# Attention and two MLPs on one core: the last batch's local v loaded from block 71 on, and two of its sets one block later

## The chip, the cores and the metric

The kernel runs on one core of one Trainium2 chip. The metric is the device time in microseconds; lower is better. Before the change three runs took 889.38, 891.51 and 893.7 us, with a median of 891.51 us. One execution was profiled; it took 892.35 us.

## The reference

The program chains three layers in float32.

```python
# attention: q, k, v are (4 batches, 8 heads, 576 positions, 64)
scores = q @ k.T / 8
rel = pos[:, None] - pos[None, :]
mask_local = (rel >= 0) & (rel < 32)                         # heads 0 to 3
mask_strided = (rel >= 0) & (pos[None, :] % 32 == pos[:, None] % 32)  # heads 4 to 7
attn = softmax(where(mask, scores, -1e9)) @ v                # x: 2304 tokens x 512
x = ((x @ w_a) * (x @ w_b)) @ w_out                          # 512 -> 1536 -> 512
h = x @ w_in                                                 # 512 -> 2048
out = (h * sigmoid(h)) @ w_out2                              # 2048 -> 512
```

The weights come as 64-bit floats and are read as pairs of 32-bit words.

## The kernel before

**Precision.** TensorE multiplies in a reduced float32 form. Each operand is therefore split into a high part (a cast, on ScalarE) and a rest (a subtraction, on VectorE), and each product is made of three matmuls. The splits are lines 775 and 776 for weights (`w<-raw`) and 793 and 794 for activations (`h<-h`, `h<-g`).

**Blocks.** The 2304 tokens are cut into groups of 512. The first 104 blocks, each of 12 matmuls of 128x512, work on group 0 through the first MLP (phase A, blocks 0 to 35), group 1 through the first MLP (blocks 36 to 71) and group 0 through the second MLP (phase B, blocks 72 to 103). In phase B a block is either an up product "i" (`ring<-y,w`, line 783, into one of two PSUM banks called ring) or a down product "p" (`acc<-w,h`, line 1568): the order is i0, i1, i2, p0, i3, p1 and so on, to i15, p13, p14, p15. So block 74 is i2, block 79 is p2, block 82 is i6, block 83 p4. What follows behind block 103 is a Strassen-like scheme for the remaining groups, which the change does not touch.

**Weights.** During the blocks the 64-bit weights are loaded (`words`, 512 KB a piece), converted by GpSimd (line 728), ScalarE (lines 744 and 702) and VectorE (line 753) to float32 (`raw`), kept in device memory (line 768) and loaded again for later blocks (`raw<-kept...`, line 693, 256 KB a piece, seven blocks ahead of use).

**Attention in the gaps.** Batch 0 is computed in a start-up stage. Batches 1 to 3 are computed between the blocks. A batch has nine units: five local ones (0 to 4; heads 0 to 3) and four strided ones (5 to 8; heads 4 to 7). They go in four sets, TOGETHER = (0, 1), (2, 3, 4), (5, 6), (7, 8). A table PLAN gives for each batch the block at which its loads begin, the block at which each set starts, and a last block for loads that belong to the next batch. For a set that starts at block s with n units, the scores (line 467, `att<-kT,qT`) stand on TensorE ahead of block s + 2; mask, maximum (lines 479, 489) and exponentials (line 501) follow in blocks s + 2 on, one unit a block; the sums are inverted (lines 524, 528) on VectorE and the probabilities normalised (line 539) on GpSimd in block s + n + 2; the transposition ("turn", line 559) stands ahead of block s + n - 1 + 6, and the values (line 608, `att<-ptl,vl` or `att<-pt,vs`) one block later. A table TURN_AT replaces the 6 for single sets: before, 7 for the first and 5 for the last set of batch 3.

**Loads of the attention.** q and k of the local heads and of the strided heads (`qld`, `kld`, line 312, 144 KB a piece, read in pieces of 128 bytes), local v (`vl`, lines 366 and 376: two loads of 32 KB, four of 128 and four of 144, read in pieces of 256 bytes) and strided v (`vs`, line 396) are issued by SP, one at a time at the start of a block. The function `spread` (line 806) distributes n issues evenly over a range of blocks. There is one buffer for `vl`; it is free for batch 3 when the second set of batch 2 has made its values, ahead of block 56.

**Order.** All instructions are issued in the order in which the Python code records them, each engine runs its own in that order, and SP's queue holds the loads of weights and of attention alike. The pieces to look at are `load_vl` (line 362), `plan_attention` (line 802) and `block` (line 848).

Of the kernel before, what the change touches and what calls it, by code (L numbers as in the profile page):

```python
# [106 lines left out]
PLAN = {  # L107
    1: (0, [2, 10, 18, 26], 36),
    2: (37, [40, 47, 55, 62], 70),
    3: (70, [73, 81, 89, 96], 0),  # L110
}
TURN_AT = {(3, 0): 7, (3, 7): 5}

STILL = 3
BETWEEN = (1, 2, 1, 2, 3, 1, 2)
# [14 lines left out]
def attention_gated_mlp_silu_mlp(  # L130
# [671 lines left out]
    def plan_attention(batch, s0, first, end):  # L802

        add = lambda at, place, f, *a: plan.setdefault((at, place), []).append((f, a))

        def spread(loads, n, s0, s1):
            for m in range(n):
                add(s0 + m * (s1 - s0) // n, "load", next, loads, None)

        starts = {us[0]: s for us, s in zip(TOGETHER, first)}  # L810
        first1 = starts[NL]
        turn1 = first1 - 1
        for one in range(4):
            add(s0 + (one if batch.b > 1 else one // 2), "prepare", batch.transpose_qk, 0, one)
            add(turn1 - 4 + one + one // 2, "prepare", batch.transpose_qk, 1, one)
        spread(batch.load_qk(1), 9, s0 + (4 if batch.b > 1 else 2), turn1 - 7)
        spread(batch.load_vs(), 4 * TAKE + 5, s0 + 4 * (batch.b > 1), first1 + 3)
        for us, s in zip(TOGETHER, first):
            others = len(us) - 1
            turn = s + others + TURN_AT.get((batch.b, us[0]), 6)  # L820
            add(s + 2, "softmax", batch.sums, *us)
            add(s + 2, "tensor", batch.scores, *us)
            for n, u in enumerate(us):
                add(s + n - others, "prepare", batch.prepare, u)
                add(s + n + 2, "mask", batch.mask, u)
                add(s + n + 2, "mask", batch.largest, u)
                add(s + n + 2, "softmax", batch.softmax, u)
                add(turn, "turned", batch.turned, u)
            add(s + others + 3, "normalise", batch.guard, us[0])
            add(s + others + 3, "normalise", batch.invert, us[0])  # L830
            for u in us:
                add(s + others + 3, "normalise", batch.normalise, u)
            add(turn, "tensor", batch.turn, *us)
            add(turn + 1, "tensor", batch.values, *us)
            add(turn + 1, "store", batch.store, *us)
        after = Batch(batch.b + 1, False)
        if after.b < B:
            spread(after.load_qk(0), 9, turn1 + 2, end)
            spread(after.load_vl(), 10, first1 + 7, end)
        return after  # L840

    def background(at, *places):
# [35 lines left out]
    with tc.manual_schedule():  # L878
# [13 lines left out]
        after = Batch(1, False)  # L892
# [96 lines left out]
        sp, hs, late, ys = {}, {}, {}, {}  # L989
# [510 lines left out]
        for ph, g in PHASES:  # L1500
# [7 lines left out]
            for kind, j in half[ph]:  # L1508
                if batch.b < B and p == PLAN[batch.b][0]:
                    batch = plan_attention(batch, *PLAN[batch.b])  # L1510
# [119 lines left out]
```

## Time and profile before

| what | value |
| --- | --- |
| runs | 889.38, 891.51, 893.7 us |
| profiled execution | 892.35 us |
| its span, first to last instruction | 890.6 us |
| TensorE busy | 878.5 us, 99% of the span |
| VectorE, ScalarE, GpSimd busy | 637.3, 541.8, 161.4 us |
| mean granted clock of TensorE | 0.988 |

The span is 1.75 us shorter than the time of the same execution. A timeline has one engine's instructions in order of time; in brackets stands how long the engine was idle before an instruction, and what ended that idle time. SP does not compute: its rows are the issues of DMA transfers, and a row's length is that of the issue, not of the transfer.

### The profile page before, as it was taken

What the parts mean: (1) busy time and instruction counts of PE and PEld (TensorE: products, weight loads), DVE (VectorE), ACT (ScalarE), POOL (GpSimd) and SP (SyncE); (2) the same over time, 40 slices, a digit from 0 to 9 for tenths busy, and PEclk for the clock granted to TensorE, in tenths of its full rate; (3) what the DMA queues carried; (4) which work ended last, traced back from release to release, by engine and by line L of the source; (5) the groups of instructions that cost most, each with busy time, mean ns of one, the idle gap of its engine ahead of it and who ended that gap; (6) DMA issues with size and microseconds to landing.
All of it is one profiled execution on the core that took longest, in us unless ns stands there. A gap on an engine that the chain in (4) does not pass through costs nothing.

```text
span 890.6 us, 16104 instructions
## 1 busy us (share of the span) xinstructions
PE 878.5 (99%) x5859; PEld 731.4 (82%) x5866; DVE 637.3 (72%) x1177; ACT 541.8 (61%) x1294; POOL 161.4 (18%) x232
## 2 busy tenths in 40 slices
PE   8899999999999999999999999999999999999998
PEld 5578788888887788999888888888888888989887
DVE  4587877767667776788776668766777697766664
ACT  4679898777777656665444344655554565455553
POOL 5655664444443200100000000000000000000000
PEclk9599999999999999999999999999999999999999
DMA  9999999798999923664122222321121342321201
GB/s 182 219 233 281 290 283 296 222 286 275 308 283 296 312 88 95 190 188 145 47 72 57 62 71 71 112 78 59 59 73 49 96 164 71 126 65 51 81 0 71
DMA packets 152977, 133.77 MB, mean 150 GB/s; under 512 B 91522, under 2 KB 114690, under 8 KB 152898
## 3 DMA queue, kind: packets, MB, share of 16 engines
q1 hardware_dynamic: 143986, 108.59, 43.3%
q0 software_dynamic: 7424, 23.34, 7.2%
q8 instruction: 46, 0.75, 0.4%
q10 hardware_dynamic: 1488, 0.82, 0.3%
q14 instruction: 33, 0.27, 0.1%
HBM read 110.16 MB, written 22.54 MB: 149 GB/s over the span
## 4 chain that ended last, share of the span: by engine, by line
PE 90%; DVE 3%; DMA 2%; ACT 2%; issue 1%; SPq 1%; POOL 1%; DVEq 0%; POOLq 0%; ACTq 0%
PE ring L783 19%; PE acc L1169 13%; PE ring L1105 12%; PE att L1105 9%; PE ring L1169 7%; PE att L1169 7%; PE acc L1105 7%; PE acc L1540 6%; PE acc L1568 4%; PE att L608 1%; PE acc L887 1%; PE att L467 1%; PE acc L783 1%; DMA raw<-kepti 1%; PE att L559 1%
## 5 line engine op out<-in xcount | busy, mean ns | idle before, releaser
L1434 DVE TENSOR_TENSOR w<-raw,w 128x512 fp32r<-128x512 f32 (+1 forms) x164 | 103.3, 642 | 14.8 <-ACT w L1433 13.9
L783 PE MATMUL ring<-x1a,w 128*128 128x256 f32 (+1 forms) x480 | 99.0, 327 | 0.0
L1433 ACT CAST w<-raw 128x512 fp32r<-128x512 f32 (+1 forms) x164 | 93.1, 581 | 7.2 <-ACT w L1433 3.0
L1105 PE MATMUL ring<-L,w 128*128 128x512 f32 x360 | 87.8, 389 | 0.0
L1218 POOL DMA_DIRECT2D out_dram<-o x12 | 6.5, 546 | 407.8 <-DVE o L1217 398.9
L1105 PEld LDWEIGHTS ring<-L,w 128*128 128x128 f32 x360 | 67.6, 188 | 14.0
L1169 PE MATMUL acc<-w,h 128*128 128x512 f32 x288 | 78.5, 391 | 0.0
L783 PEld LDWEIGHTS ring<-x1a,w 128*128 128x128 f32 x480 | 71.5, 190 | 7.8
L1540 PE MATMUL acc<-h,w 128*128 128x512 f32 x288 | 70.5, 394 | 0.6 <-ACT h L793 0.4
L793 ACT CAST h<-h 128x512 fp32r<-128x512 f32 (+1 forms) x48 | 27.2, 566 | 72.0 <-DVE h L1142 40.5
L776 DVE TENSOR_TENSOR w<-raw,w 128x512 fp32r<-128x512 f32 x80 | 61.7, 775 | 10.9 <-ACT w L775 10.2
L1540 PEld LDWEIGHTS acc<-h,w 128*128 128x128 f32 x288 | 53.2, 188 | 12.3 <-ACT h L793 0.6
L1169 PEld LDWEIGHTS acc<-w,h 128*128 128x128 f32 x288 | 53.6, 188 | 9.4 <-DVE h L794 0.4
L728 POOL TENSOR_SCALAR raw<-words 128x512 f16<-128x512 uint8 x56 | 51.2, 915 | 42.7 <-DMA words<-in_moe_w_in_dram 9.2
L783 PE MATMUL ring<-x,w 128*128 128x512 f32 x240 | 58.0, 394 | 0.1
L1169 PE MATMUL acc<-h,w 128*128 128x256 f32 (+1 forms) x288 | 53.5, 336 | 0.0
L783 PEld LDWEIGHTS ring<-x,w 128*128 128x128 f32 x240 | 44.4, 188 | 10.2 <-DVE w L776 1.1
L1169 PE MATMUL ring<-w,h 128*128 128x512 f32 x192 | 52.0, 391 | 0.0
L775 ACT CAST w<-raw 128x512 fp32r<-128x512 f32 x80 | 49.6, 623 | 1.2 <-DMA raw<-kepti 1.2
L1169 PEld LDWEIGHTS acc<-h,w 128*128 128x128 f32 x288 | 45.2, 190 | 5.7
L794 DVE TENSOR_TENSOR h<-h,h 128x512 fp32r<-128x512 f32 (+1 forms) x48 | 30.6, 637 | 26.4 <-ACT h L793 26.4
L1169 PE MATMUL att<-w,h 128*128 128x512 f32 x192 | 49.3, 391 | 0.0
(264 smaller groups left out, 1918.3 us busy)
## 6 DMA issues: line engine op xcount, KB each, us to landing
raw<-keptp SPq DMA_DIRECT2D x64, 256.0 KB
words<-in_moe_w_out_dram SPq DMA_DIRECT2D x28, 512.0 KB
raw<-kepti SPq DMA_DIRECT2D x48, 256.0 KB
raw<-kepto SPq DMA_DIRECT2D x45, 256.0 KB
words<-in_moe_w_in_dram SPq DMA_DIRECT2D x16, 512.0 KB
raw<-keptb SPq DMA_DIRECT2D x32, 256.0 KB
raw<-kepta SPq DMA_DIRECT2D x31, 256.0 KB
words<-in_moe_w_a_dram SPq DMA_DIRECT2D x12, 512.0 KB
```

The costliest lines, as they stand in the source:

```text
L728: nc.gpsimd.tensor_scalar(out=halves_of(made[c], F16, 1), in0=bytes_of(words[c], 8, 7), scalar1=-TINY, scalar2=127.5 * TINY, op0=ALU.mult, ...
L775: nc.scalar.copy(out=o[:, 0], in_=t)
L776: nc.vector.tensor_tensor(out=o[:, 1], in0=t, in1=o[:, 0].bitcast(F32), op=ALU.subtract)
L783: nc.tensor.matmul(ps[:, :T], lhsT=w[:, wi, c * P:(c + 1) * P], rhs=x[:, xi, c, :T], start=(c == 0 and wi == 0 and xi == 0), stop=(c == CC ...
L793: nc.scalar.copy(out=o[:, 0, :T], in_=t32[:, :T])
L794: nc.vector.tensor_tensor(out=o[:, 1, :T], in0=t32[:, :T], in1=o[:, 0, :T].bitcast(F32), op=ALU.subtract)
L1105: nc.tensor.matmul(self.acc[acc], lhsT=w[:, wi, (2 * part + c) * P:(2 * part + c + 1) * P], rhs=x[:, xi, c], start=(begin and c == 0 and m ...
L1169: nc.tensor.matmul(o, lhsT=lhsT, rhs=rhs, start=(first and wi == 0 and xi == 0), stop=(last and wi == 1))
L1433: nc.scalar.copy(out=o[:, 0, cols], in_=t)
L1434: nc.vector.tensor_tensor(out=o[:, 1, cols], in0=t, in1=o[:, 0, cols].bitcast(F32), op=ALU.subtract)
L1540: nc.tensor.matmul(accs[d], lhsT=w[:, wi, d * P:(d + 1) * P], rhs=h[:, xi], start=(j == 0 and wi == 0 and xi == 0), stop=(j == N1 - 1 and ...
L1568: nc.tensor.matmul(accs[t][:, :DM], lhsT=h[:, xi, t * P:(t + 1) * P], rhs=w[:, wi, :], start=(j == 0 and wi == 0 and xi == 0), stop=(j == ...
```

## The change

Three things are edited. The second and the third set of batch 3 start one block later (81 to 82 and 89 to 90). The third set's turn comes five blocks behind instead of six, so it stays ahead of block 96 and its values ahead of block 97. The loads of batch 3's local v, which were spread over blocks 62 to 69, are spread from block 71 on, one a block to block 79 (two in block 71). Since the loads of strided q, k and v are spread up to a block that depends on the third set's start, some of these move back by a block too.

```diff
 PLAN = {
     1: (0, [2, 10, 18, 26], 36),
     2: (37, [40, 47, 55, 62], 70),
-    3: (70, [73, 81, 89, 96], 0),
+    3: (70, [73, 82, 90, 96], 0),
 }
-TURN_AT = {(3, 0): 7, (3, 7): 5}
+TURN_AT = {(3, 0): 7, (3, 5): 5, (3, 7): 5}
...
         if after.b < B:
             spread(after.load_qk(0), 9, turn1 + 2, end)
-            spread(after.load_vl(), 10, first1 + 7, end)
+            late = end + 1 if after.b == 3 else first1 + 7
+            spread(after.load_vl(), 10, late, late + 9 if after.b == 3 else end)
         return after
```

`first1` is the block at which the third set of the batch before starts (55), `end` its last block for loads (70). Lines behind the edit have numbers higher by one in the changed kernel. A small float32 matmul of the attention (lines 467 and 608) stands once in the order below and twice in the trace, so 40 rows of scores there are 80 in the timeline.

SP, blocks 77 to 79: the last k and strided-v loads around the words load of block 78, before.

```order
L674 DMA words<-in_moe_w_out_dram 128x1024
L693 DMA raw<-kepti_3062 128x512
L312 DMA kld<-in_k_dram 32x36x32
L396 DMA vs<-in_v_dram 18x10x64
L674 DMA words<-in_moe_w_out_dram 128x1024
L693 DMA raw<-keptp_3102 128x512
L312 DMA kld<-in_k_dram 32x36x32
L396 DMA vs<-in_v_dram 18x10x64
```

The same place in the changed order, up to the last load of local v.

```order
L396 DMA vs<-in_v_dram 18x10x64
L674 DMA words<-in_moe_w_out_dram 128x1024
L693 DMA raw<-kepti_3062 128x512
L376 DMA vl<-in_v_dram 64x9x64
L312 DMA kld<-in_k_dram 32x36x32
L396 DMA vs<-in_v_dram 18x10x64
L674 DMA words<-in_moe_w_out_dram 128x1024
L693 DMA raw<-keptp_3102 128x512
L376 DMA vl<-in_v_dram 64x9x64
L312 DMA kld<-in_k_dram 32x36x32
```

Ahead of each block's first load now stands one of local v; the last one, in block 79, stands behind the words and the raw load of block 78, and the k loads have moved back by one place.

TensorE, from the values of the first set (`vl` with `ptl_120` and `ptl_121`) to the scores of the second, before.

```order
L608 MATMUL att<-ptl_120,vl 64x32 x16
L608 MATMUL att<-ptl_121,vl 64x32 x16
L783 MATMUL ring<-y,w 128x512 x12
L467 MATMUL att<-kT,qT 32x64 x40
L1568 MATMUL acc_3799<-w,h 128x512 x3
L1568 MATMUL acc_3800<-w,h 128x512 x3
L1568 MATMUL acc_3801<-w,h 128x512 x3
L1568 MATMUL acc_3802<-w,h 128x512 x3
```

The same place in the changed order.

```order
L608 MATMUL att<-ptl_120,vl 64x32 x16
L608 MATMUL att<-ptl_121,vl 64x32 x16
L783 MATMUL ring<-y,w 128x512 x12
L1569 MATMUL acc_3791<-w,h 128x512 x3
L1569 MATMUL acc_3792<-w,h 128x512 x3
L1569 MATMUL acc_3793<-w,h 128x512 x3
L1569 MATMUL acc_3794<-w,h 128x512 x3
L467 MATMUL att<-kT,qT 32x64 x40
```

Block 83, the twelve matmuls into the four acc banks, has moved from behind the second set's scores to in front of them.

VectorE, from the second unit's mask and maximum in the third set to its reciprocal, before: `g` is the gate of a weight block, `su` and `rs` the sums and their reciprocals.

```order
L479 SCALAR_TENSOR_TENSOR sm<-att,mask_str 128x162 x2
L489 TENSOR_REDUCE nm<-sm 128x6
L776 TENSOR_TENSOR w<-raw,w 128x512
L1532 SCALAR_TENSOR_TENSOR g_4643<-th,ring 128x512
L794 TENSOR_TENSOR h<-g_4643,h 128x512
L524 TENSOR_SCALAR su<-su 128x12
L528 RECIPROCAL rs<-su 128x12
L776 TENSOR_TENSOR w<-raw,w 128x512 x2
```

The same place in the changed order.

```order
L1533 SCALAR_TENSOR_TENSOR g_4632<-th,ring 128x512
L794 TENSOR_TENSOR h<-g_4632,h 128x512
L479 SCALAR_TENSOR_TENSOR sm<-att,mask_str 128x162 x2
L489 TENSOR_REDUCE nm<-sm 128x6
L776 TENSOR_TENSOR w<-raw,w 128x512
L524 TENSOR_SCALAR su<-su 128x12
L528 RECIPROCAL rs<-su 128x12
L776 TENSOR_TENSOR w<-raw,w 128x512
L1533 SCALAR_TENSOR_TENSOR g_4689<-th,ring 128x512
```

The mask and the maximum have moved from ahead of block 92's gate and split to behind them; the reciprocal still stands ahead of block 94's gate, now close behind the maximum.

## Rows read from the trace of the kernel before

**Rows 1.** The page: busy time of TensorE, DMA share in 40 slices, instruction queue.

```profile
PE 878.5 (99%) x5859; PEld 731.4 (82%) x5866; DVE 637.3 (72%) x1177; ACT 541.8 (61%) x1294; POOL 161.4 (18%) x232
...
DMA  9999999798999923664122222321121342321201
...
q8 instruction: 46, 0.75, 0.4%
```

**Rows 2.** Windows of the span: first column the stretch, second its length, then PE busy.

```profile
0.00:45.00 45.00, 39.36 (x562) 25.60 (x568) 23.03 (x78) 25.35 (x118) 27.28 (x49) 0.77 0.93 202
...
550.00:890.00 340.00, 336.90 (x1555) 287.31 (x1553) 241.46 (x437) 181.99 (x355) 4.31 (x8) 1.00 0.24 77
```

**Rows 3.** Timeline of PE: start, length, line, output<-inputs, count, idle time before it.

```profile
271.24 3.06 PE L783 MATMUL ring<-y,w 128*128 128x512 f32 x12 [0.75 <-DVE g L1532]
...
286.07 2.88 PE L1568 MATMUL acc<-w,h 128*128 128x512 f32 x12
...
289.65 2.57 PE L783 MATMUL ring<-y,w 128*128 128x512 f32 x10 [0.25 <-DVE w L776]
...
295.36 1.14 PE L608 MATMUL att<-ptl,vl 64*64 64x32 f32 x64
...
299.37 0.76 PE L467 MATMUL att<-kT,qT 64*32 64x64 f32 x49
301.01 0.46 PE L467 MATMUL att<-kT,qT 64*32 64x64 f32 x31 [0.88 <-issue]
...
317.85 0.71 PE L559 MATMUL att<-ident,prs 128*128 128x128 f32 x5
```

**Rows 4.** Timeline of ACT, 262 to 312 us.

```profile
266.71 0.62 ACT L775 CAST w<-raw 128x512 fp32r<-128x512 f32 x1 [1.20 <-DMA raw<-kepti]
```

**Rows 5.** Timeline of SP's DMA issues, 225 to 325 us.

```profile
236.93 2.33 SPq L366 DMA_DIRECT2D vl<-in_v_dram  x2
...
260.47 0.49 SPq L693 DMA_DIRECT2D raw<-kepti  x1
...
262.33 0.60 SPq L376 DMA_DIRECT2D vl<-in_v_dram  x1
...
274.62 1.22 SPq L312 DMA_DIRECT2D qld<-in_q_dram  x2
...
292.16 0.55 SPq L674 DMA_DIRECT2D words<-in_moe_w_out_dram  x1
292.81 0.38 SPq L693 DMA_DIRECT2D raw<-keptp  x1
```

**Rows 6.** Timeline of POOL, 225 to 365 us.

```profile
298.26 0.83 POOL L728 TENSOR_SCALAR raw<-words 128x512 f16<-128x512 uint8 x1 [1.40 <-DMA words<-in_moe_w_out_dram]
...
313.87 1.99 POOL L539 TENSOR_TENSOR prs<-prs,rs 128x256 f32<-128x256 f32 x3 [7.71 <-DVE rs L528]
337.84 2.14 POOL L539 TENSOR_TENSOR prs<-prs,rs 128x324 f32<-128x324 f32 x2 [21.97 <-DVE rs L528]
```

**Rows 7.** Windows with and without local-v loads: the last two columns are DMA share and GB/s.

```profile
237.00:263.00 26.00, 26.00 (x233) 21.25 (x234) 16.02 (x28) 19.20 (x54) 10.31 (x14) 1.00 1.08 310
264.00:274.00 10.00, 9.25 (x41) 7.23 (x39) 8.05 (x12) 6.77 (x12) 3.82 (x6) 1.00 1.08 333
274.00:293.00 19.00, 18.75 (x145) 15.04 (x144) 13.46 (x25) 13.49 (x37) 7.40 (x9) 1.00 0.99 248
```

**Rows 8.** The tile vl: its transfers from issue to landing.

```profile
DMA to landing us min/median/max: 3.2/5.4/8.0
```

**Rows 9.** Timeline of DVE, 317 to 366 us.

```profile
337.44 0.23 DVE L528 RECIPROCAL rs<-su 128x12 f32<-128x12 f32 x1
```

**Rows 10.** Timeline of PE, 317 to 372 us.

```profile
325.47 0.92 PE L467 MATMUL att<-kT,qT 64*64 64x54 f32 x48
...
340.06 0.82 PE L559 MATMUL att<-ident,prs 128*118 128x128 f32 x6
```

## The prediction

> **What bounds the kernel now.** I read the page first: TensorE is busy 878.5 us of a span of 890.6, 99% [rows 1], so no change can gain more than the 12 us in which it is idle. The windows of the span say where those are: 45.00 - 39.36 = 5.6 us in the start-up and 340.00 - 336.90 = 3.1 us behind 550 us [rows 2], both out of the change's reach. The timeline of TensorE then shows three holes in the stretch that the change touches: 0.75, 0.25 and 0.88 us, 1.88 us together [rows 3]. That sum is the most that the change can give, 0.2% of the time; what it can cost is not bounded in this way.
>
> The first hole has a history. A load of a piece of the weights issued at 260.47 us, between two of the local-v loads [rows 5], lets ScalarE wait 1.20 us and start its cast only at 266.71 [rows 4], 6.2 us after the issue. VectorE is late behind it, frees the ring bank late, and TensorE waits 0.75 us at 271.24 [rows 3]. The second hole, 0.25 us, ends with a split weight, so again with the feeding of weights. The third, 0.88 us, falls in the middle of the second set's 80 score matmuls: 49 run, then nothing that the profile can name, then 31 [rows 3]. It stands behind 64 value matmuls and 49 score matmuls that took 1.14 and 0.76 us, so many instructions in little time, and the page shows an instruction queue of 46 packets with 0.75 MB [rows 1], 16 KB each, that shares the DMA engines. I take it to be late code.
>
> The DMA digits show that the transfers, too, are near their limit in slices of 22.3 us up to the fourteenth, that is to 312 us [rows 1]. The coarser windows agree: 310 GB/s from 237 to 263 us, while batch 3's ten local-v loads are issued, 333 from 264 to 274, and only 248 at a DMA share of 0.99 from 274 to 293, where eight q and k loads with their 128-byte pieces go out [rows 7].
>
> **Part 1: local v goes from blocks 62 to 69 to blocks 71 to 79.** Ten issues leave SP between 236.93 and about 263 us [rows 5] and take the same ten places among the loads of the first blocks of phase B. What is removed: two of 32 KB, four of 128 and four of 144, 1152 KB in all, ahead of the weights. At 310 GB/s that is 3.8 us of DMA time, more than the 1.20 us by which ScalarE was late, so I take away the whole first hole, -0.75, and the second with it, -0.25 (at worst both stay: 0).
>
> What it adds is a wait. The values of the first set read all of local v with their first eight matmuls. Before, it landed some 30 us ahead. Now its last load is an instruction of block 79, three blocks ahead of the values. SP does not issue it when TensorE begins block 79. SP runs in its own order: behind the words load issued at 292.16 and the raw load at 292.81 [rows 5] comes the last local-v load in the changed order, while TensorE starts those values at 295.36 [rows 3], and without the first two holes at 295.36 - 1.00 = 294.36. Queued behind that wait on TensorE are the values themselves, blocks 82 and 83 and the second set's scores: all of its work, so a microsecond of wait is a microsecond of time.
>
> When does the load land? The row nearest to it is the words load of 292.16: GpSimd, waiting for it for 1.40 us, starts at 298.26 [rows 6], 6.1 us after the issue. In the changed order the last local-v load is the second one behind that same load, and up to there the queue has carried the same transfers as before, less one k load (144 KB, 0.46 us at 310 GB/s), which goes out later. If the DMA engines stay saturated, the order of transfers doesn't change when the last of them is done, so 298.2 - 0.5 = 297.7 us, and TensorE waits 297.7 - 294.36 = +3.3 us. From below: SP runs ahead by the 1.20 us that ScalarE no longer loses, issues at 292.16 - 1.2 = 291.0, and the load needs 3.2 us, the shortest shown for this tile [rows 8]: 294.2, no wait, 0. From above: the engines idle before 274 us, where the weights alone don't fill them, and the six loads from block 74 on (832 KB, less 144 KB of k) go at the 248 GB/s of that stretch: 2.8 us later than 293.2, where the raw load's issue ends, and 6.1 us to land: 302.1, a wait of 7.7. I take 3.3, since its row lies next to the load in the queue, and keep 0 and 7.7. Weights that SP issues behind local v come later by up to the same amount, but TensorE's wait gives them that time back.
>
> A rule of the Trainium skill speaks against the new place ("DMA: Bandwidth & Descriptors", section "Why small descriptors are slow (HBM only)"): a 256-byte piece costs 11 cycles instead of 8. Local v is read in 256-byte pieces, so by that rule the six loads from block 74 on would cost about a quarter more, as an estimate 0.6 us, and the wait would be 3.9 in place of 3.3. The trace agrees only in part: with these loads in the queue the rate was 310 GB/s against 333 without [rows 7], 7% less.
>
> **Part 2: the second set one block later.** Same matmuls, another place: block 83 of 24 weight matmuls now runs between the values and the 80 scores. If the third hole is late code, the 2.7 us of that block give the fetch its time, and a wait for local v does so as well: -0.88 (it stays: 0). The rest of the set keeps its distance of seven blocks from scores to values; GpSimd's normalising began at 313.87 and took 1.99, and the turn came at 317.85 [rows 6, 3], so 2.0 us of slack, and both move by the same block. The turn and the values also move one block: 0.
>
> The Trainium skill ("Runtime: NRT & Kernel Launch", section "Instruction fetch mechanics") holds the cost of crossing into the next 16 KiB of code to be mostly hidden. By that the hole is not code, and would stay: the sum would be 0.88 higher. The size per packet agrees with the page of the profile; the hole, with no other releaser, does not look hidden, so I keep -0.88.
>
> **Part 3: the third set one block later, its turn where it was.** The distance from start to turn shrinks by a block. Before, scores began at 325.47, the reciprocal at 337.44, GpSimd normalised from 337.84 to 339.98, and TensorE turned from 340.06 [rows 9, 6, 10]: already with almost nothing to spare. But the chain had waits in it that the later start eats up: VectorE did the reciprocal behind a weight block's gate and split. Laid out from the durations, scores now end 2.7 us later, the two softmaxes follow at 330.2 and 336.0, the reciprocal ends near 338.4, and GpSimd is done by 340.6 in place of 339.98. TensorE needs the second half only 0.3 us into the turn. That is +0.3; from below 0, from above one whole block, 2.7, if a gate slips ahead of the softmax.
>
> **Sum.** -0.75 - 0.25 - 0.88 + 3.3 + 0.3 = +1.7 us. The profiled execution took 892.35 us, so 894.1; it lay 0.84 above the median of the runs, 891.51, and on that scale I predict 893.2.
>
> **The rivals.**
> - No wait at the values: SP is so far ahead by block 79 that local v lands by 294.4. For it, SP's pace before 274 us is set by free buffers and not by the DMA, so it starts the stretch unburdened; against it, the raw load of 292.81, the last issue of block 78, is 6.7 us behind the start of block 79 on TensorE at 286.07 [rows 5, 3]. Then -1.88 + 0.3: 889.9.
> - Slower than before: the wait for the last local-v load grows to 6 us or more, since eight q and k loads and now six local-v loads are squeezed into 19 us at 248 GB/s [rows 7]. It decides from a wait of 1.88 - 0.3 = 1.6 us on whether the kernel loses at all, and from about 6 whether the loss can be told. With 7: -1.88 + 7 + 0.3 = +5.4, 896.9.
> - The third set's turn slips by a block, with local v in time: -1.88 + 2.7, 892.3. For it, 0.1 us of slack before [rows 6, 10]; against it, the layout above.
> - The change does not do what it says: the holes stay (late code and late weights are found at other places), and local v lands in time: 891.5.
>
> **How the numbers follow.** Forecast 0.42 (its own range 891.4 to 895.9, for waits from 1.5 to 6); no wait 0.30; longer wait 0.14; third set 0.06; nothing 0.08. What differs by under 0.5%, 4.5 us, can't be told from no change in a measurement of this kernel. Only the longer wait goes beyond that, most of it: slower 0.13. A gain of 4.5 us is more than the holes hold; 0.03 is left for what I have not seen. Same: 0.84. The range goes from no wait, less 0.9 for the scatter of the runs, 889.0, to the longer wait at 897.0.
>
> **What would show it.** Right: the profile after has a TensorE wait in front of the first set's values, its releaser a DMA or nothing named, of 1.5 to 6 us, no hole near 270 us and none in the second set's scores. Part 1 is wrong if those values follow block 81 without a hole; part 2 if the scores still break off; part 3 if TensorE waits over 1 us for GpSimd at the third set's turn. A gain of more than 1.9 us would mean that time came from outside these blocks.

## The result and the profile after

The changed kernel takes 899.91 us (median of 6 runs, 899.22 to 902.77) against 891.13 for the kernel before (6 runs); the ratio is 1.0098, with an interval of 1.0082 to 1.0114. It is 8.8 us slower. The prediction said 893.2, in a range up to 897.0.

The profiled execution took 902.77 us with a span of 901.0, the slowest of the six, so its parts add up to a little more than the medians: its span is 10.4 us longer than the one before. The timeline of TensorE after shows nearly all of it in one place (start, length, line, output<-inputs, count, idle time before):

```profile
286.10 2.88 PE L1569 MATMUL acc<-w,h 128*128 128x512 f32 x12
...
289.66 2.59 PE L783 MATMUL ring<-y,w 128*128 128x512 f32 x10 [0.23 <-DVE w L776]
...
295.40 0.42 PE L608 MATMUL att<-ptl,vl 64*64 64x32 f32 x12
298.73 0.30 PE L608 MATMUL att<-ptl,vl 64*64 64x32 f32 x2 [2.91 <-DMA vl<-in_v_dram]
304.08 1.70 PE L608 MATMUL att<-ptl,vl 64*64 64x32 f32 x50 [5.05 <-DMA vl<-in_v_dram]
305.71 4.80 PE L783 MATMUL ring<-y,w 128*128 128x512 f32 x12
310.35 2.91 PE L1569 MATMUL acc<-w,h 128*128 128x512 f32 x12
313.19 1.04 PE L467 MATMUL att<-kT,qT 64*32 64x64 f32 x80
...
350.10 1.17 PE L559 MATMUL att<-ident,prs 128*118 128x128 f32 x6
```

The values of the first set begin at 295.40, before at 295.36 [rows 3], although a hole of 0.75 us ahead of them is gone: in this execution TensorE is busy for 38.90 of the first 45 us and was for 39.36, so the start-up took that gain away. After six of them (twelve rows) TensorE waits 2.91 us for a load of local v, and after the seventh 5.05 us for the next: 8.0 us. Then everything is slow for a while: the last 50 value matmuls take 1.70 us, and the weight block i6 4.80, where such a block took 3.06 at 271.24 before [rows 3]. From the start of the values to the start of i6 it is 10.31 us and was 1.07; from there to what follows i6 (block p4 after, the scores before) 4.64 and was 2.94. That is 9.24 + 1.70. The scores at 313.19 no longer break off, and what lies between i6 and the third set's turn is 0.94 us shorter. So from the values to that turn: +9.24 + 1.70 - 0.94 = +10.0 of the 10.4. The turn itself takes 0.35 us more, 1.17 against 0.82 [rows 10].

The windows of 2 us after (last three columns: granted clock of TensorE, DMA share, GB/s) say why the work behind the wait is slow:

```profile
296.00:298.00 2.00, 0.00 (x0) 0.00 (x0) 1.32 (x2) 0.62 (x1) 0.89 (x2) 1.00 1.11 302
298.00:300.00 2.00, 0.30 (x2) 0.19 (x2) 0.98 (x2) 1.80 (x3) 0.44 (x1) 0.83 0.59 105
300.00:302.00 2.00, 0.00 (x0) 0.00 (x0) 0.69 (x1) 0.00 (x0) 0.01 (x1) 0.50 0.96 365
...
306.00:308.00 2.00, 2.00 (x5) 1.53 (x5) 0.69 (x1) 1.99 (x5) 0.00 (x0) 0.50 1.17 248
...
310.00:312.00 2.00, 2.00 (x11) 1.61 (x10) 0.69 (x1) 0.70 (x2) 0.00 (x0) 1.00 0.98 316
```

TensorE stands still from 296 to 304 apart from two matmuls; the granted clock falls to 0.50, that is 1.2 GHz, from 300 us on, and is back at 1.00, 2.4 GHz, by 310. The values and i6 run in between: 1.3 + 1.7 = 3.0 us on top of the waits of 8.0.

SP's issues after show where the last load of local v stands in time:

```profile
267.49 0.32 SPq L693 DMA_DIRECT2D raw<-keptp  x1
267.87 1.35 SPq L366 DMA_DIRECT2D vl<-in_v_dram  x2
...
274.62 0.61 SPq L376 DMA_DIRECT2D vl<-in_v_dram  x1
...
292.34 0.61 SPq L376 DMA_DIRECT2D vl<-in_v_dram  x1
...
293.72 2.98 SPq L396 DMA_DIRECT2D vs<-in_v_dram  x1
296.81 1.23 SPq L674 DMA_DIRECT2D words<-in_moe_w_out_dram  x1
...
299.52 0.61 SPq L376 DMA_DIRECT2D vl<-in_v_dram  x1
```

The words load of block 78 goes out at 296.81 and was issued at 292.16 before; the last local-v load follows it, at 299.52, and TensorE goes on at 304.08, 4.6 us later. Landing itself took no longer than thought: the issue is late. Ahead of the words load, the issue of one strided-v load takes 2.98 us. It is no single event: from 274.62 on, the lengths of SP's issues add up to 23.2 of the 24.8 us until the raw load in front of the last local-v load is out. So SP hardly pauses for buffers there; it is its issues that take the time.

The coarse windows that answer to [rows 7]:

```profile
237.00:263.00 26.00, 26.00 (x233) 20.98 (x232) 15.62 (x29) 19.21 (x54) 10.58 (x15) 1.00 1.04 337
264.00:274.00 10.00, 10.00 (x46) 8.18 (x44) 7.69 (x12) 7.29 (x13) 2.56 (x5) 1.00 0.72 208
274.00:293.00 19.00, 18.77 (x145) 15.01 (x143) 13.73 (x25) 13.49 (x37) 6.91 (x9) 1.00 1.02 268
293.00:312.00 19.00, 11.04 (x95) 8.79 (x94) 6.69 (x10) 8.23 (x18) 2.66 (x4) 0.73 1.00 267
```

Without local v in front, the engines move 337 GB/s up to 263 us, and then, from 264 to 274, only 208 where there were 333. Up to 267.49 SP stands still for 6.6 us, until VectorE frees a buffer for a raw load, and the first local-v load is queued behind that raw load. From 274 on they are at a share of 1.02 but at 268 GB/s, little more than the 248 of before.

### The profile page after: what moved, and what is told of

Same layout as the page of the kernel before. It is cut to its first block, busy times and chain, and to the rows that moved or that the text cites. A ratio compares the mean times of both kernels' runs of the same rounds, so it can differ in the third digit from the quotient of the medians.

```text
span 901.0 us, 16101 instructions
## 1 busy us (share of the span) xinstructions
PE 881.8 (98%) x5859; PEld 733.7 (81%) x5866; DVE 637.6 (71%) x1177; ACT 541.9 (60%) x1294; POOL 161.3 (18%) x232
## 4 chain that ended last, share of the span: by engine, by line
PE 86%; ACT 5%; DVE 4%; DMA 3%; issue 1%; SPq 1%; POOL 1%; ACTq 0%; DVEq 0%; POOLq 0%
PE ring L783 17%; PE acc L1170 13%; PE ring L1106 12%; PE att L1106 9%; PE ring L1170 7%; PE att L1170 7%; PE acc L1106 7%; PE acc L1541 6%; PE acc L1569 3%; PE att L608 1%; ACT w L775 1%; ACT prs L501 1%; PE att L467 1%; PE acc L783 1%; DMA kld<-in_k_dram 1%
## 5 line engine op out<-in xcount | busy, mean ns | idle before, releaser
L1435 DVE TENSOR_TENSOR w<-raw,w 128x512 fp32r<-128x512 f32 (+1 forms) x164 | 103.4, 642 | 14.8 <-ACT w L1434 14.1
```

Source lines behind the costliest of these rows:

```text
L1435: nc.vector.tensor_tensor(out=o[:, 1, cols], in0=t, in1=o[:, 0, cols].bitcast(F32), op=ALU.subtract)
```

## The experiments

Theory A is that the wait for the last local-v load is the whole loss. It is split into A1 (the load is late because SP comes to it late, behind q and k) and A2 (the DMA engines are full, whoever issues, and whenever), and theory C adds the clock. Rival B puts a part of the loss on the sets that were moved. Ratios are against the kernel before on the same chip. Block 79 begins at 282.93 us in the earliest of these traces and at 286.10 in the latest, so an issue is placed by its distance from the start of block 79 in its own trace: 13.4 us for the last local-v load of the change (299.52 - 286.10).

**Only local v late.** PLAN and TURN_AT as before, the edit of `spread` as in the change.

```diff
-    3: (70, [73, 82, 90, 96], 0),
+    3: (70, [73, 81, 89, 96], 0),
...
-TURN_AT = {(3, 0): 7, (3, 5): 5, (3, 7): 5}
+TURN_AT = {(3, 0): 7, (3, 7): 5}
```

> Local v is loaded from block 71 on as in the change; the sets start where they did before (81, 89, six blocks to the third turn). Theory A (the wait of the first set's values for the last local-v load is the whole loss): the two waits in front of those values stay, 6 to 8 us together, and the time is 898 to 901 us, 8 to 10 us above before. Rival B (a part of the loss comes from the sets that start later): under 896 us.

Measured: 901.03 us, ratio 1.0109 (1.0088 to 1.0129). TensorE's timeline at the first set's values:

```profile
293.34 0.42 PE L608 MATMUL att<-ptl,vl 64*64 64x32 f32 x12
298.58 0.42 PE L608 MATMUL att<-ptl,vl 64*64 64x32 f32 x2 [4.81 <-DMA vl<-in_v_dram]
302.76 1.70 PE L608 MATMUL att<-ptl,vl 64*64 64x32 f32 x50 [3.76 <-DMA vl<-in_v_dram]
...
309.06 1.04 PE L467 MATMUL att<-kT,qT 64*32 64x64 f32 x80
```

The waits are 4.81 and 3.76 us, 8.6 together. This edit alone gives the whole loss; B is out. The second set's 80 scores run in one piece here too, although they stand right behind i6 as before.

**Only the sets moved.** Local v in blocks 62 to 69.

```diff
-            late = end + 1 if after.b == 3 else first1 + 7
-            spread(after.load_vl(), 10, late, late + 9 if after.b == 3 else end)
+            late = first1 + 7
+            spread(after.load_vl(), 10, late, end)
```

> The second and third set of batch 3 start one block later with the five-block turn as in the change; local v is loaded in blocks 62 to 69 as before. Theory A: no wait for local v; the holes near 270 and 289 us stay as in the kernel before, the break in the second set's scores is gone (-0.9 us), the third turn waits under 0.5 us: 889.5 to 891.5 us. Rival B: 894 us or more, with a wait of TensorE at one of the two moved sets.

Measured: 889.70 us, ratio 0.9981 (0.9967 to 0.9994): a little faster than before. The timeline of TensorE has the first set's values and the second's scores without a break, and the third set's turn with one:

```profile
270.49 3.02 PE L783 MATMUL ring<-y,w 128*128 128x512 f32 x12 [0.30 <-DVE g L1533]
...
294.59 1.14 PE L608 MATMUL att<-ptl,vl 64*64 64x32 f32 x64
...
301.32 1.04 PE L467 MATMUL att<-kT,qT 64*32 64x64 f32 x80
...
338.91 0.54 PE L559 MATMUL att<-ident,prs 128*118 128x128 f32 x3 [0.15 <-POOL prs L539]
```

The 80 scores run in one piece, as forecast for part 2, and GpSimd holds the second half of the third turn for 0.15 us, as sized in part 3. The hole at 270 us is there again, 0.30 us this time.

**The values a block later.**

```diff
-TURN_AT = {(3, 0): 7, (3, 5): 5, (3, 7): 5}
+TURN_AT = {(3, 0): 8, (3, 5): 5, (3, 7): 5}
```

> The change, but the first set of batch 3 is turned eight blocks behind its start instead of seven, so that its values stand ahead of block 83 and not 82. Theory A: block 82 now runs during the wait, which gets one block (2.7 us) shorter: 896 to 898 us. If the late load is itself held up by what TensorE does there (buffers that blocks 82 and on free), it lands later too and the gain is under 1 us: 899 us or more.

Measured: 897.61 us, ratio 1.0076 (1.0056 to 1.0095), 2.3 us below the change, as theory A expected, though the intervals of the two ratios overlap.

```profile
298.11 0.69 PE L608 MATMUL att<-ptl,vl 64*64 64x32 f32 x14 [2.97 <-ACT ptl L568]
301.17 1.70 PE L608 MATMUL att<-ptl,vl 64*64 64x32 f32 x50 [2.37 <-DMA vl<-in_v_dram]
```

TensorE still waits 2.97 and 2.37 us, 5.3 in place of 8.0: one block of work less in the wait. The second wait is for local v. The first is for the copies of the turned probabilities, and ScalarE's timeline says why they are late:

```profile
296.00 0.62 ACT L775 CAST w<-raw 128x512 fp32r<-128x512 f32 x1 [2.21 <-DMA raw<-kepti]
...
297.70 0.63 ACT L568 COPY ptl<-att 128x256 f32<-128x256 f32 x2
```

The cast in front of them waited 2.21 us for a piece of the weights. So it is not local v alone that comes late: what SP issues behind it is late as well, and here that shows.

**The late loads issued by GpSimd.** At the same blocks, past SP's queue.

```diff
+        def issue(loads, queue):
+            feed[0] = queue
+            next(loads, None)
+            feed[0] = nc.sync
...
-            spread(after.load_vl(), 10, late, late + 9 if after.b == 3 else end)
+            spread(after.load_vl(), 10, late, late + 9 if after.b == 3 else end, nc.gpsimd if after.b == 3 else nc.sync)
```

> The change, with the ten late local-v loads of batch 3 issued by GpSimd instead of SP, at the same blocks. Theory A1 (the load is late because SP issues it late, behind the q, k and strided-v loads in its queue): issued near the start of block 79 and landed about 5 us later, it meets the values: no wait or under 1.5 us, 889 to 892 us. Rival A2 (the DMA engines are full, whoever issues): the values still wait 4 us or more, 895 to 900 us.

Measured: 895.19 us, ratio 1.0048 (1.0029 to 1.0066). GpSimd's last issue of local v, and TensorE at block 79 and at the values:

```profile
290.09 0.80 POOL L376 DMA_DIRECT2D vl<-in_v_dram  x1
```

```profile
283.80 2.88 PE L1574 MATMUL acc<-w,h 128*128 128x512 f32 x12
...
295.21 0.30 PE L608 MATMUL att<-ptl,vl 64*64 64x32 f32 x2 [1.62 <-DMA vl<-in_v_dram]
297.00 1.49 PE L608 MATMUL att<-ptl,vl 64*64 64x32 f32 x50 [1.50 <-DMA vl<-in_v_dram]
```

The last load is issued 6.3 us behind the start of block 79, 7.1 us nearer to it than in the change, yet it lands only by 297.0, 6.9 us after its issue, and TensorE waits 3.1 us. Neither forecast fits whole: the time is at the lower end of A2's range, the wait below its 4 us. Past SP's queue 4.8 of the 8.0 us of wait go. That fits a load that is late because of its place in that queue, but this run does not say how much of the wait comes from there, since the edit changes the transfers too: the page counts the 1.2 MB of these loads under queue q0, software_dynamic, in 512 packets, where the change has them under q1, hardware_dynamic, in 4768.

**The q and k loads behind local v.** The eight loads of strided q and k go out in blocks 80 to 84, behind the last local-v load.

```diff
-        spread(batch.load_qk(1), 9, s0 + (4 if batch.b > 1 else 2), turn1 - 7)
+        spread(batch.load_qk(1), 9, s0 + (10 if batch.b == 3 else 4 if batch.b > 1 else 2), turn1 - (4 if batch.b == 3 else 7))
```

> The change, with the eight loads of batch 3's strided q and k issued in blocks 80 to 84 instead of 74 to 81, behind the last local-v load. Theory A1 (the q and k loads with their 128-byte pieces ahead in SP's queue are what makes the last local-v load late): it is issued by 291 us and landed by 296, the wait falls under 2 us: 889 to 893 us, unless the transposes of the late q then wait. Rival (the words and raw loads, which wait for free buffers, hold SP): SP issues the last local-v load as late as in the change, 297 us or later: 897 us or more.

Measured: 890.98 us, ratio 1.0006 (0.9994 to 1.0018). The same ten late local-v loads, in the same blocks, and no loss. SP's last local-v issue, TensorE at block 79 and at the values, and the two windows of the transfers:

```profile
290.76 0.61 SPq L376 DMA_DIRECT2D vl<-in_v_dram  x1
```

```profile
285.16 2.88 PE L1569 MATMUL acc<-w,h 128*128 128x512 f32 x12
...
294.54 0.43 PE L608 MATMUL att<-ptl,vl 64*64 64x32 f32 x14
295.64 1.00 PE L608 MATMUL att<-ptl,vl 64*64 64x32 f32 x50 [0.68 <-DMA vl<-in_v_dram]
```

```profile
264.00:274.00 10.00, 10.00 (x105) 8.09 (x104) 8.30 (x13) 6.85 (x13) 2.12 (x3) 1.00 0.61 187
274.00:293.00 19.00, 18.71 (x106) 15.10 (x89) 13.57 (x25) 14.24 (x37) 7.01 (x10) 1.00 1.05 309
```

SP issues the last load 5.6 us behind the start of block 79, 7.8 us nearer to it than in the change, and TensorE waits 0.68 us for it. From the fifth of the ten local-v loads, at 273.74 (274.62 in the change), to the raw load in front of the tenth SP is issuing for 8.7 of 17.0 us, where it was 23.2 of 24.8. The five strided-v loads in that stretch take 2.3 us to issue and took 7.4. What makes an issue longer is not shown; the share of the engines, 1.05 here and 1.02 in the change, does not tell the two apart. With local v and weights and without q and k, the engines move 309 GB/s from 274 to 293 us in place of 268. From 264 to 274 they are as idle as in the change, 187 GB/s. So the idle time ahead of 274 us does not make the load late by itself; the six q and k loads in front of it do. Whether that comes from their 128-byte pieces or from six more loads in the queue, no run separates.

**Local v from block 68, 65 and 70.** Three kernels, with the sets moved as in the change.

```diff
-            late = end + 1 if after.b == 3 else first1 + 7
+            late = 68 if after.b == 3 else first1 + 7
```

The others have 65 and `end` (70) in place of 68.

> The change, with batch 3's local v issued in blocks 68 to 76 instead of 71 to 79. In the trace after, SP issues what stands at block 76 at about 285 to 289 us, and a load needs 5 to 6 us. Theory A1 (SP's lateness grows from block 74 on with the q and k loads): the last load lands at 290 to 294, before the values at 295: 889 to 891.5 us, no wait. Rival A2 (the DMA engines' load in this stretch sets it, three blocks change little): a wait of 3 us or more, 894 us or more.

> The change, with batch 3's local v issued in blocks 65 to 73, still later than the 62 to 69 of before. Theory A: no wait for local v, and the two small holes of weights near 270 and 289 us come out between those of before and of the change: 888.5 to 890.5 us, as with the sets alone (889.7). Rival (any load of local v in the stretch delays the weights for phase B): holes of 1 us or more at the first blocks of phase B, 891 us or more.

> The change with local v in blocks 70 to 78, one block earlier. Theory A1: the last load is issued where the ninth of the change was, near 292 to 295 us, and lands 5 to 6 us later, at 298 to 300: a wait of 3 to 5 us, 893 to 897 us, so between the 890.8 of blocks 68 to 76 and the 899.9 of 71 to 79. If the loss came from a single event of the last block (the strided-v and words issues that took 2.98 and 1.23 us there), the wait is nearly gone: under 892 us.

Measured: from 68, 890.80 us, ratio 1.0002 (0.9987 to 1.0018); from 65, 889.12 us, ratio 0.9987 (0.9979 to 0.9996); from 70, 895.70 us, ratio 1.0048 (1.0033 to 1.0064). From 68 the last load is issued at 283.64, and the values run through:

```profile
283.64 0.61 SPq L376 DMA_DIRECT2D vl<-in_v_dram  x1
```

```profile
293.78 1.14 PE L608 MATMUL att<-ptl,vl 64*64 64x32 f32 x64
```

From 65, both values and scores are in one piece:

```profile
292.58 1.14 PE L608 MATMUL att<-ptl,vl 64*64 64x32 f32 x64
...
299.32 1.04 PE L467 MATMUL att<-kT,qT 64*32 64x64 f32 x80
```

From 70, a single wait of 5.78 us is left, a little more than forecast, and behind it the slow values and a block i6 of 4.25 us:

```profile
299.07 1.70 PE L608 MATMUL att<-ptl,vl 64*64 64x32 f32 x50 [5.78 <-DMA vl<-in_v_dram]
300.70 4.25 PE L783 MATMUL ring<-y,w 128*128 128x512 f32 x12
```

So the loss goes from nothing to 8.8 us over three blocks, 68 to 71, and it is no mishap of one issue. From 70 to 71 the medians differ by 4.2 us, more than the 2.7 of a block; in the traces the waits grow by 2.2, and what is lost behind them by 0.85.

**The wait filled.** Constant matmuls ahead of the values keep TensorE at work, 34 in the first kernel and 44 in the second.

```diff
+        def fill(n):
+            bank = att_tile(False)
+            one = nc.const_aps.tensor(1.0, [P, 512], BF16)
+            for _ in range(n):
+                nc.tensor.matmul(bank, lhsT=one[:, :P], rhs=one, start=True, stop=True)
...
+            if (batch.b, us[0]) == (3, 0):
+                add(turn + 1, "tensor", fill, 34)
             add(turn + 1, "tensor", batch.values, *us)
```

> The change, with 34 bf16 matmuls of a constant (128x512, written to an attention bank that the values then overwrite) ahead of the first set's values; they take some 7.3 us at the high clock, which is less than the 8.0 us of the two waits. Theory C (some 2.6 us of the loss is TensorE's clock, which falls to 1.2 GHz in the wait and slows the values and the block behind them): granted clock 1.00 through the wait, block 82 in 3.0 us and not 4.8, and the time is 896.5 to 898.5 us. Rival (the wait alone is the loss): 899 to 901 us.

> As the filled wait, with 44 constant matmuls instead of 34: 9.5 us at the high clock, so that they reach to where the last local-v load lands and no idle time is left in which the clock can fall (with 34, 1.88 us of idle time were left and block 82 still ran at 1.2 GHz for the most part). Theory C (the low clock costs some 2.6 us): granted clock 1.00 throughout, block 82 in 3.0 us, 896.5 to 898 us, although more is issued. Rival (the clock costs nothing that is not lost anyway): 899 to 901 us.

Measured: 897.83 us with 34, ratio 1.0090 (1.0074 to 1.0106), and 898.58 with 44, ratio 1.0080 (1.0066 to 1.0093; the kernel before was 891.96 in that set of runs). With 34 (the trace has 33 of them), then with 44:

```profile
293.69 7.61 PE L810 MATMUL att<-const-bfloat16-1.0 128*128 128x512 bf16 x33
...
303.79 1.00 PE L608 MATMUL att<-ptl,vl 64*64 64x32 f32 x50 [1.88 <-DMA vl<-in_v_dram]
304.72 4.61 PE L783 MATMUL ring<-y,w 128*128 128x512 f32 x12
```

```profile
292.14 9.80 PE L810 MATMUL att<-const-bfloat16-1.0 128*128 128x512 bf16 x44
302.05 1.25 PE L608 MATMUL att<-ptl,vl 64*64 64x32 f32 x64
303.22 3.01 PE L783 MATMUL ring<-y,w 128*128 128x512 f32 x12
```

With 34 a wait of 1.88 us is left, and i6 still takes 4.61 us. With 44 there is none: the 64 values take 1.25 us and i6 3.01. The trace so shows that the slow stretch follows the idle time and is gone without it. In the time the gain can't be told: both intervals overlap that of the change, the first time lies in theory C's range without the fast i6 that C expected, and the second lies between C's range and the rival's. The longer filling takes 9.80 us of its own, more than the wait of 8.0 that it replaces; in the traces it is 14.1 us from its start to the end of i6, and 15.1 in the change from the start of the values. That work behind the wait is slow is read from the trace of the change; that keeping the clock up pays is left open.

## Why the prediction was wrong

**The bound and the holes were right.** No change here could gain more than 1.88 us, and the sets alone, or local v from block 65, gain 1.6 and 1.9 in the medians (889.70 and 889.12 against 891.26 and 891.01 for the kernel before; the ratios make it 1.7 and 1.2).

**The first hole went, the second stayed.** No hole is left near 270 us in any kernel with local v late; with the sets alone 0.30 us of it stayed. The second, at 289.66, is 0.23 us and was 0.25 [rows 3]. It stays in every kernel tried, 0.22 to 0.34 us, local v early or late, so it was no matter of local v.

**The scores' hole went**, by 0.94 us and with the sets alone too. It also went with local v alone late, where no block was put in between but TensorE had waited 8.6 us in front. That is what part 2 said of both; that the cause was late code has not been shown.

**The third set's turn** was sized rightly at +0.3: 0.15 us of wait in the kernel with the sets alone. In the change GpSimd works from 348.79,

```profile
348.79 1.89 POOL L539 TENSOR_TENSOR prs<-prs,rs 128x324 f32<-128x324 f32 x2 [19.30 <-ACT w L775]
```

to 350.68, and the turn at 350.10 takes 0.35 us longer than before.

**The step that failed is the landing of the last local-v load.** I took it from the words load beside it [rows 5, 6], on the premise "if the DMA engines stay saturated, the order of transfers doesn't change when the last of them is done", and got 297.7 us; it was some 304.0. The wait of +3.3 us was 8.0, and even the upper bound of 7.7 was too low. From issue to landing the load was quicker than the 6.1 us taken, 4.6. The issue was late: 299.52, where the raw load in front of it had been out at 293.2 before.

The premise fails at two places. The engines were not saturated: from 264 to 274 us they moved 208 GB/s and not 333, which the upper bound had allowed for. And the bytes added did not tell the time: from 274.62 to the end of that raw load SP needed 18.6 us before and 24.8 after, 6.3 more, for which the upper bound had 2.8, worked out from 688 KB at 248 GB/s. Before, the ten local-v loads went out among three k loads and the large weight loads; after, six of them went out among six q and k loads of 128-byte pieces, and there SP issued one load after the other and fell behind. With q and k out of the way the same load came 7.8 us sooner.

The kernel was on the side of the rival with the longer wait, to which I gave 0.14; its argument, the squeeze of eight and six loads into 19 us, was the one that the runs bear out. The wait even passed the 7 us that the rival was reckoned with. The side estimate of 0.6 us for the 256-byte pieces was too small by its own figures, three eighths more being 1.0 us, but either is far from the 4.7 us by which the wait was missed.

**A term was missing**: what TensorE loses behind a wait. The granted clock fell to 0.50, 1.2 GHz, and the work behind the wait took 3.0 us more in this execution. In the sum a microsecond of wait was a microsecond of time; here it was 1.37. Not all of that is the clock: with q and k behind local v the values, broken once by a wait of 0.68 us, took 0.28 us more than the wait explains, at a granted clock of 1.00. As an estimate from this, the two breaks are 0.6 of the 3.0 us.

**The warning was in the distances**: before, the last load lay in block 69, thirteen blocks ahead of the values, after, three; and SP was 6.7 us, two and a half blocks, behind TensorE at that place before anything was added [rows 3, 5]. The prediction had both, but set the 6.7 us only against the rival without a wait, and its forecast did not let it grow with the loads added; it was 13.4.

## What to carry to other kernels

When a load moves along an issue queue, forecast the time of its issue from what stands around it at the new place, not from the bytes in total: here six q and k loads ahead of it were worth 7.8 us, and a stretch in which the engines then idled made no room in the stretch to which the loads went. The distance between a load and its reader must hold the queue's lag at that place, the lag that the new loads add, and the landing; here 13.4 us of lag (299.52 against block 79's 286.10 on TensorE) and 4.6 of landing, against the 9.3 us from the start of block 79 to the values. A wait on TensorE can cost more than its length: here 8.0 us of waiting cost 10.9, with the granted clock at 0.50 behind it.

## What was not expected of the hardware

- GpSimd issued the last local-v load 6.3 us behind the start of block 79 and it landed 6.9 us later, while SP's own, issued 13.4 us behind it in the change, took 4.6: a load that passes SP's queue was not landed faster.
- The issue of one strided-v load, 45 KB, took SP 2.98 us in the change, and 0.3 to 0.6 us where q and k stood behind.
- The loss is steep: 890.80, 895.70 and 899.91 us for local v from block 68, 70 and 71.
- In the waits of 2.91 and 5.05 us the granted clock fell to 0.50, and it was back at 1.00 in the window from 310, with TensorE at work again since 304.08.
